# Moving the second unit's queries and norm, and closing the last tile in column halves

## The chip, the cores and the metric

The kernel runs on one core of a Trainium2 chip. The metric is the device time of one execution in microseconds. Before the change it is 1306.41 us, the median of three runs (1306.41 to 1306.56).

## The reference

The reference is a transformer block with modulation. A condition vector c gives six rows (`sa, ca, ga, sb, cb, gb`). Attention runs over 2048 queries and a cache of 2048 keys, with 32 query heads and 8 key and value heads; a gated spatial MLP follows:

```python
mod = (silu(c) @ w_mod)              # 6 rows of 512: sa, ca, ga, sb, cb, gb
h = layernorm(x) * (1 + ca) + sa     # x: 2048 x 512
q = (h @ wq)                         # 32 heads of 128; 4 query heads share a key head
p = softmax(q k^T / sqrt(128))
x = x + ga * ((p v) @ wo)
h = layernorm(x) * (1 + cb) + sb
z = gelu(h @ w_in)                   # 2048 x 1792
z1, z2 = z[:, :896], layernorm(z[:, 896:])
g = w_sp @ z2 + b_sp                 # w_sp: 2048 x 2048
out = x + gb * ((z1 * g) @ w_out)
```

All inputs and the output are bf16.

## The kernel before

The work is an order written out by hand (`tc.manual_schedule()`): each engine and each DMA queue gets its instructions in the order in which the program emits them, and semaphores tie the engines together. The DMAs of this part are all issued by SP, one after the other; the output is written by DMAs that ACT issues.

**Attention.** The 2048 rows of x are 16 tiles of 128 rows, and four tiles are a chunk (`CT = 4`). A unit `u` is one key head and one tile of queries with four query heads: 128 units, unit 0 to 15 for the first key head. The main loop steps through `it`, with eight slots `i` in each. In a slot the program emits, in this order: what was entered for that slot with `at(it, slot, fn)`; the scores of unit `it` (`qk`, L1068: two matmuls of 512 columns into a two-bank PSUM tile `s_ps`, then one exponential of 128x1024 on ACT, L1075); one part of the product with v of an earlier unit (`pv`, L1124: eight matmuls of 129 columns); and what was entered in `fill[it, slot]`, which is mostly query projections (`qproj`, L967). At the end of each group of query heads a cast on DVE (L978) brings the projected queries from PSUM into `qT`. `pv` of unit 0 runs in the last four slots of unit 0 and the even slots of unit 1; after each two heads DVE takes a reciprocal (L1135) and writes the normalised output `onorm` (L1136), and after the fourth head SP transposes it into `oT` (L1147). The projection with wo uses `oT` some units later.

**The first layernorm.** The first chunk's tiles are normalised in the preamble and in unit 0. For the second chunk, `ln1_at(1, (0, 7), (1, 2), (2, 2))` enters four steps: the statistics of its four tiles at slot 7 of unit 0 (`ln1_stats`, L697 and L698 on DVE, then L678 and L682 on POOL for the reciprocal deviation); the normalisation of the four tiles at slot 2 of unit 1 (`ln1_norm`, L686 on DVE); four DMA transposes into `hT` at slot 3 (`ln1_dma`, L836 on SP); and the modulation at slot 2 of unit 2 (`ln1_dma_mod`, four operations on DVE, L805, each over all four tiles). The projection of the second chunk's queries starts in `fill[2, 5]`. Between these, SP loads `wmod_b` (2 MB, L1312, the tile is called `wsp` in the profile), which is entered at slot 4 of unit 1 and is first used in unit 6.

**Queries of unit 2 and 3.** `rest_q` projects tiles 2 and 3 of the first chunk: sixteen matmuls of 256 columns in two groups of two heads, put into the slots 1 to 6 of unit 1. Unit 2's scores need both groups' casts.

**The end.** The last 512 rows of the spatial product are computed as 384 and then 128 columns. For each of seven f the last 128 columns take sixteen matmuls (L1545), one for the bias (L1565), and DVE's product with z1 into `yT` (L1573). The last tile's output projection `o2_mm` (L1578) takes seven matmuls of 512 columns, one for each f: f = 0 to 2 within the loop, f = 3 to 6 behind it. `finish_tile` then multiplies by `gb_rows` from PSUM into `tmp` (L1590), adds x into `yout` (L1591), both on DVE, and ACT issues the DMA (L1592). A flag `redo`, computed earlier, decides at the very end (L1643) whether a general path runs; here it doesn't.

Of the kernel before, what the change touches and what calls it, by code (L numbers as in the profile page):

```python
# [10 lines left out]
BF16 = mybir.dt.bfloat16  # L11
FP32 = mybir.dt.float32
ACT = mybir.ActivationFunctionType
ALU = mybir.AluOpType
AX = mybir.AxisListType
P = 128
# [559 lines left out]
def kernel(  # L576
# [19 lines left out]
    nc = tc.nc  # L596
    _, S, D = A_x.shape
# [7 lines left out]
    NT = S // P  # L605
    NDT = D // P
    NKT = SK // P
    NFT = FH // P
    NCH = S // 512
    CT = 512 // P  # L610
# [8 lines left out]
    out_dram = out[0].rearrange("(t p) d -> p t d", p=P)  # L619
# [26 lines left out]
    x_sb = res.tile([P, NT, D], BF16, name="x_sb")  # L646
    ga_rows = res.tile([P, D], FP32, name="ga_rows")
    gb_rows = res.tile([P, D], FP32, name="gb_rows")
# [20 lines left out]
    def bank(name):  # L669
        return psum.tile([P, 512], FP32, name=name)  # L670
# [4 lines left out]
    def rstd_of(mv, n, tag):  # L675

        ve = stat.tile([P, CT], FP32, name=f"ve_{tag}")
        nc.gpsimd.tensor_scalar(  # L678
            out=ve[:, :n], in0=mv[:, :, 1], scalar1=LN_EPS, scalar2=None, op0=ALU.add
        )  # L680
        rstd = stat.tile([P, CT], FP32, name=f"rstd_{tag}")
        nc.gpsimd.tensor_tensor(out=rstd[:, :n], in0=ve[:, :n], in1=mhalf[:, :n], op=ALU.pow)  # L682
        return rstd

    def normalise(dst, src, mv, rstd):
        nc.vector.tensor_scalar(  # L686
            out=dst,
            in0=src,
            scalar1=mv,
            scalar2=rstd,  # L690
            op0=ALU.subtract,
            op1=ALU.mult,
        )

    def ln_stats(mv, j, src):
        st = stat.tile([P, 1, nc.vector.BN_STATS_DIM], FP32, name="bnst")
        nc.vector.bn_stats(out=st[:, 0, :], in_=src)  # L697
        nc.vector.bn_aggr(out=mv[:, j, :], in_=st[:])  # L698
# [87 lines left out]
    def ln1_stats(j0, n):  # L786
        for j in range(j0, j0 + n):
            ln_stats(mv1, j, x_sb[:, j, :])
        return rstd_of(mv1[:, j0 : j0 + n, :], n, "ln1")

    def ln1_norm(j0, n, rstd):
        xns = []
        for j in range(j0, j0 + n):
            xn = res.tile([P, D], BF16, name="xn1", bufs=4)
            normalise(xn[:], x_sb[:, j, :], mv1[:, j, 0:1], rstd[:, j - j0 : j - j0 + 1])
            xns.append(xn)
        return xns

    def hT_of(ch):
        if ch not in hTs:  # L800
            hTs[ch] = res.tile([P, NDT, 512], BF16, name="hT", bufs=NCH)
        return hTs[ch]

    def ln1_mod(dst, src, dt, engine=nc.vector):
        engine.tensor_scalar(  # L805
            out=dst,
            in0=src,
            scalar1=modc[:, NDT + dt : NDT + dt + 1],
            scalar2=modc[:, dt : dt + 1],
            op0=ALU.mult,  # L810
            op1=ALU.add,
        )
# [20 lines left out]
    def ln1_dma(j0, n, xns):  # L833
        hT = hT_of(j0 // CT)
        for jj in range(n):
            nc.sync.dma_start_transpose(out=hT[:, :, jj * P : (jj + 1) * P], in_=xns[jj][:])  # L836

    def ln1_dma_mod(ch):
        for dt in range(NDT):
            ln1_mod(hTs[ch][:, dt, :], hTs[ch][:, dt, :], dt)  # L840
# [79 lines left out]
    for dt in range(NDT):  # L920
        dst, src = hTs[0][:, dt, 0:P], xT0[:, dt * P : (dt + 1) * P]
        if dt == 1:
            nc.scalar.activation(
                out=dst,
                in_=src,
# [29 lines left out]
    def qproj(b, heads, c0, n, banks=("misc", "misc")):  # L955

        g, ch = divmod(b, NCH)
        if b not in qTs:
            qTs[b] = early.tile([P, REP, 512], BF16, name="qT")
        one = n * len(heads) <= 512  # L960
        ps = {}

        def mm(hh, dt):
            if dt == 0 and (not one or hh == heads[0]):
                ps[0] = bank(banks[hh % 2])
            o0 = (hh - heads[0]) * n if one else 0
            nc.tensor.matmul(  # L967
                ps[0][:, o0 : o0 + n],
                lhsT=wqs[g][:, dt, hh * DH : (hh + 1) * DH],
                rhs=hTs[ch][:, dt, c0 : c0 + n],  # L970
                start=(dt == 0),
                stop=(dt == NDT - 1),
            )
            if dt == NDT - 1 and (not one or hh == heads[-1]):
                hs = heads if one else [hh]
                dst = qTs[b][:, hs[0] : hs[-1] + 1, c0 : c0 + n]
                src = ps[0][:, 0 : len(hs) * n].rearrange("p (h q) -> p h q", q=n)
                nc.vector.tensor_copy(out=dst, in_=src)  # L978

        return [lambda hh=hh, dt=dt: mm(hh, dt) for hh in heads for dt in range(NDT)]  # L980

    first = {}
# [30 lines left out]
    def at(it, slot, fn):  # L1013
        later.setdefault((it, slot), []).append(fn)
# [265 lines left out]
    fill = {}  # L1280
# [16 lines left out]
    fill[0, 4], fill[0, 5] = next_q[0:8], next_q[8:16]  # L1297
    rest_q = qproj(0, [0, 1], 2 * P, 2 * P) + qproj(0, [2, 3], 2 * P, 2 * P)
    for i in range(6):
        fill[1, i + 1] = rest_q[(8 * i + 2) // 3 : (8 * i + 10) // 3]  # L1300

    def ln1_at(ch, stats, norm, turn):
        st = {}
        at(*stats, lambda: st.update(r=ln1_stats(ch * CT, CT)))
        at(*norm, lambda: st.update(x=ln1_norm(ch * CT, CT, st["r"])))
        at(norm[0], norm[1] + 1, lambda: ln1_dma(ch * CT, CT, st["x"]))
        at(*turn, lambda: ln1_dma_mod(ch))

    ln1_at(1, (0, 7), (1, 2), (2, 2))
    ln1_at(2, (2, 4), (3, 1), (4, 5))  # L1310
    ln1_at(3, (3, 5), (4, 1), (5, 5))
    at(1, 4, lambda: nc.sync.dma_start(out=wmod_b, in_=wmod_dram[:, :, 2 * D : NMOD]))  # L1312
# [34 lines left out]
    for g in range(1, HKV):  # L1347
# [7 lines left out]
        last = it - 1  # L1355
        for from_it, load in loads:
# [3 lines left out]
            last = next(u for u in pauses if u >= it + from_it and u > last)  # L1360
# [94 lines left out]
    for it in range(NU + 6):  # L1455
# [37 lines left out]
        if it == NU + 2:  # L1493
            free_b.close()
            mlp = fast.enter_context(tc.tile_pool(name="mlp", bufs=1, side="right"))
            zs["z1T"] = mlp.tile([P, NFT, S], BF16, name="z1T")
            wout_sb = mlp.tile([P, NFT, D], BF16, name="wout_sb")
# [14 lines left out]
    for f in range(NFT):  # L1512
# [6 lines left out]
        out=ok1[:], in0=rall[:], scalar1=1.0 / SAFE, scalar2=None, op0=ALU.is_ge  # L1519
# [8 lines left out]
        out=bad[:], in0=okm[:], scalar1=-1.0, scalar2=1.0, op0=ALU.mult, op1=ALU.add  # L1528
# [48 lines left out]
    def o2_mm(dst, yT, jj, f):  # L1577
        nc.tensor.matmul(  # L1578
            dst,
            lhsT=yT[:, f, jj * P : (jj + 1) * P],  # L1580
            rhs=wout_sb[:, f, :],
            start=(f == 0),
            stop=(f == NFT - 1),
        )

    def finish_tile(t, jj, src):
        j = t * CT + jj
        tmp = mlp.tile([P, D], FP32, name="tmp", bufs=2)[:].bitcast(BF16)[:, 0:D]
        yout = mlp.tile([P, D], BF16, name="yout", bufs=2)
        nc.vector.tensor_tensor(out=tmp[:], in0=src, in1=gb_rows[:], op=ALU.mult)  # L1590
        nc.vector.tensor_tensor(out=yout[:], in0=tmp[:], in1=x_sb[:, j, :], op=ALU.add)  # L1591
        nc.scalar.dma_start(out=out_dram[:, j, :], in_=yout[:])  # L1592
# [3 lines left out]
    def o2_tile(t, jj):  # L1596
        o2 = bank("o_ps")
        for f in range(NFT):
            o2_mm(o2[:], yTs[t], jj, f)
        finish_tile(t, jj, o2[:])  # L1600

    last = NCH - 1
# [16 lines left out]
    o2_last = [acc[jj // 2][:, (jj % 2) * 512 : (jj % 2 + 1) * 512] for jj in range(CT)]  # L1619
    yT = yTs[last]  # L1620
    for f in range(NFT):
        spatial(last, yT, f, 0, n_a)
        if f < CT:
            o2_tile(last - 1, f)
        if f > 0:
            for jj in range(CT - 1):
                o2_mm(o2_last[jj], yT, jj, f - 1)
    redo = nc.values_load(flag[0:1, 0:1], min_val=0, max_val=P)
    for f in range(NFT):
        spatial(last, yT, f, n_a, P, bias_by_pe=True)  # L1630
        if f == 0:
            for jj in range(CT - 1):
                o2_mm(o2_last[jj], yT, jj, NFT - 1)
        elif f < CT:
            o2_mm(o2_last[CT - 1], yT, CT - 1, f - 1)
        if f % 2 == 0 and f < 2 * (CT - 1):
            finish_tile(last, f // 2, o2_last[f // 2])
    for f in range(CT - 1, NFT):
        o2_mm(o2_last[CT - 1], yT, CT - 1, f)
    finish_tile(last, CT - 1, o2_last[CT - 1])  # L1640
    fast.close()

    with tc.If(redo != 0):  # L1643
# [34 lines left out]
```

## Time and profile before

| | value |
|---|---|
| median of 3 runs | 1306.41 us |
| the profiled execution's own time | 1306.41 us |
| its span, first to last instruction | 1304.6 us |
| time around the span | 1.8 us |
| PE busy | 1287.9 us, 99% of the span |
| ACT busy | 1113.4 us, 85% |
| DVE busy | 684.1 us, 52% |
| POOL busy | 57.4 us, 4% |
| mean granted TensorE clock | 0.999 |

PE is the matrix engine, PEld its weight loads, ACT the scalar engine, DVE the vector engine, POOL GpSimd and SP the engine whose queue issues DMAs; a q behind an engine's name means its queue. In a timeline line the columns are the start in us from the begin of the span, the length in us, the engine, the line of the kernel, the operation, the tile written and the tiles read, the shape, and the number of instructions merged into the line; brackets give the idle time before the first of them and what ended it. Durations of matmuls are those of one alone (0.38 us at 512 columns), while back to back they start 0.215 us apart.

### The profile page before, as it was taken

The page shows a single profiled execution, that of the slowest core. Times are in us where ns is not written, and L with a number is a line of the kernel's source. Part 1 is how long each engine was busy: PE and PEld are TensorE (multiplying, and loading weights), DVE is VectorE, ACT ScalarE, POOL GpSimd, SP SyncE. Part 2 cuts the span into 40 slices and gives each one's busy share as a digit, 9 for nine tenths or more (in the row PEclk, how much of TensorE's full clock was granted, in tenths as well). Part 3 has the DMA queues.
Part 4 walks back from the last instruction along what each step waited for, and adds up shares of the span by engine and source line. Part 5 has one row for each costly group of instructions (what it writes and reads, how often), then busy time and mean ns, then how long its engine had stood idle before and what let it go on. Part 6 is the DMA issues. An engine that isn't in the chain of part 4 may idle for free.

```text
span 1304.6 us, 22478 instructions
## 1 busy us (share of the span) xinstructions
PE 1287.9 (99%) x8472; PEld 698.1 (54%) x8626; DVE 684.1 (52%) x1772; ACT 1113.4 (85%) x1683; POOL 57.4 (4%) x93
## 2 busy tenths in 40 slices
PE   8999999999999999999999999999999999999998
PEld 6655555555555555555555555555555556644445
DVE  5635445544554455445544554455445566784443
ACT  7999999999999999999999999999999998650000
POOL 1000000000000000000000000000000133410000
PEclk9999999999999999999999999999999999999999
DMA  7899899999999999999999999999999983264300
GB/s 187 183 198 189 157 190 182 190 170 189 181 194 168 188 173 184 183 181 183 185 188 173 183 187 189 172 185 176 177 198 163 168 151 90 49 137 98 81 21 31
DMA packets 774982, 211.19 MB, mean 162 GB/s; under 512 B 759248, under 2 KB 773200, under 8 KB 774864
## 3 DMA queue, kind: packets, MB, share of 16 engines
q1 hardware_dynamic: 772416, 207.55, 87.0%
q10 hardware_dynamic: 2448, 2.10, 0.5%
q8 instruction: 70, 1.15, 0.4%
q14 instruction: 48, 0.39, 0.1%
HBM read 21.37 MB, written 2.10 MB: 18 GB/s over the span
## 4 chain that ended last, share of the span: by engine, by line
PE 95%; DVE 2%; ACT 1%; DMA 1%; issue 1%; POOL 0%; SPq 0%; ACTq 0%
PE s_ps L1031 21%; PE o_ps L1103 20%; PE o_ps L1124 14%; PE s_ps L1068 13%; PE misc L1181 8%; PE misc L967 8%; PE misc L1545 7%; PE o_ps L1578 1%; PE s_ps L1411 1%; PE s_ps L1372 1%; DVE stz L1394 1%; PE s_ps L1578 0%; DMA wmod_a<-in_w_mod_dram 0%; ACT pT L1075 0%; DMA xnT<-xn 0%
## 5 line engine op out<-in xcount | busy, mean ns | idle before, releaser
L1031 PE MATMUL s_ps<-kT,qT 128*128 128x512 bf16 x1219 | 364.9, 379 | 2.3
L1038 ACT ACTIVATE win_sb<-s_ps 128x1024 bf16<-128x1024 f32 x312 | 319.2, 1024 | 3.8 <-PE s_ps L1031 0.7
L1103 PE MATMUL o_ps<-pT,v 128*128 128x512 bf16 x909 | 272.5, 379 | 1.3
L1174 DVE SCALAR_TENSOR_TENSOR xacc<-misc,rall,xacc 128x512 f32<-128x512 f32 x304 | 227.4, 748 | 68.2 <-PE misc L1181 60.7
L1068 PE MATMUL s_ps<-qT,kT 128*128 128x512 bf16 x784 | 233.2, 379 | 1.9 <-ACT pT L1075 1.1
L1075 ACT ACTIVATE pT<-s_ps 128x1024 bf16<-128x1024 f32 x216 | 217.8, 1025 | 12.9 <-PE s_ps L1068 4.9
L1038 ACT ACTIVATE pn<-s_ps 128x1024 bf16<-128x1024 f32 x208 | 213.0, 1024 | 2.0 <-PE s_ps L1031 0.5
L1103 PEld LDWEIGHTS <-v 128*128 128x128 bf16 x1248 | 122.1, 98 | 147.3
L1075 ACT ACTIVATE wsp<-s_ps 128x1024 bf16<-128x1024 f32 x176 | 179.9, 1024 | 12.1 <-PE s_ps L1068 4.2
L1181 PE MATMUL misc<-wo_g,oT 128*128 128x512 bf16 x479 | 181.5, 379 | 1.0
L967 PE MATMUL misc<-hT,wq_g 128*128 128x512 bf16 (+2 forms) x499 | 179.6, 370 | 0.5
L1031 PEld LDWEIGHTS <-qT 128*128 128x128 bf16 x1248 | 121.5, 98 | 109.4 <-issue 0.4
L978 DVE CAST qT<-misc 128x512 bf16<-128x512 f32 x127 | 87.2, 687 | 151.2 <-PE misc L967 151.2
L1124 PEld LDWEIGHTS <-pT 128*128 128x128 bf16 x1792 | 119.6, 98 | 50.5
L1092 DVE TENSOR_TENSOR tot<-rs 128x1 f32<-128x1 f32 x312 | 48.4, 155 | 171.5 <-ACT win_sb L1038 115.2
L1124 PE MATMUL o_ps<-v,pT 128*128 128x129 bf16 x1792 | 137.5, 220 | 0.6
L1068 PEld LDWEIGHTS <-kT 128*128 128x128 bf16 x784 | 75.6, 98 | 83.0 <-DVE qT L978 1.5
L1124 PEld LDWEIGHTS <-wsp 128*128 128x128 bf16 x1408 | 94.3, 98 | 41.5
L1124 PE MATMUL o_ps<-v,wsp 128*128 128x129 bf16 x1408 | 108.5, 220 | 0.5
L1038 ACT ACTIVATE wmod_a<-s_ps 128x1024 bf16<-128x1024 f32 x104 | 106.4, 1024 | 0.4 <-PE s_ps L1031 0.4
L1545 PE MATMUL misc<-wsp,z 128*128 128x512 bf16 (+2 forms) x554 | 100.1, 336 | 0.4
L1103 PE MATMUL o_ps<-wsp,v 128*128 128x512 bf16 x292 | 87.8, 379 | 0.4
(111 smaller groups left out, 874.3 us busy)
## 6 DMA issues: line engine op xcount, KB each, us to landing
wo_g<-in_A_wo_dram SPq DMA_DIRECT2D x8, 512.0 KB, 5.0
wq_g<-in_A_wq_dram SPq DMA_DIRECT2D x7, 512.0 KB, 4.0
v<-in_A_v_cache_dram SPq DMA_DIRECT2D x7, 512.0 KB, 4.5
wsp<-in_w_mod_dram SPq DMA_DIRECT2D x1, 2048.0 KB, 8.7
out_dram<-yout ACTq DMA_DIRECT2D x16, 128.0 KB, 1.7
pT<-win_sb SPq DMA_TRANSPOSE x117, 4.8
win_sb<-in_B_w_in_dram SPq DMA_DIRECT2D x1, 1792.0 KB, 8.0
x_sb<-in_A_x_dram SPq DMA_DIRECT2D x3, 512.0 KB, 7.0
```

The source lines that it names most:

```text
L967: nc.tensor.matmul(ps[0][:, o0 : o0 + n], lhsT=wqs[g][:, dt, hh * DH : (hh + 1) * DH], rhs=hTs[ch][:, dt, c0 : c0 + n], start=(dt == 0), s ...
L978: nc.vector.tensor_copy(out=dst, in_=src)
L1031: nc.tensor.matmul(s_ps[:, c * 512 : (c + 1) * 512], lhsT=qTs[b][:, hh, jj * P : (jj + 1) * P], rhs=groups[g]["kT"][:, k0 : k0 + 512], sta ...
L1038: nc.scalar.activation(out=rows_of(u, hh)[:, half * HK : (half + 1) * HK], in_=s_ps[:], func=ACT.Exp, scale=inv_sqrt_dh, accum_out=rsums[u ...
L1068: nc.tensor.matmul(s_ps[:, h * 512 : (h + 1) * 512].rearrange("p (r q) -> p r q", r=REP), lhsT=groups[g]["kT"][:, kt * P : (kt + 1) * P], ...
L1075: nc.scalar.activation(out=pTs[u][:, 2 * i : 2 * i + 2, :], in_=s_ps[:].rearrange("p (k q) -> p k q", k=2), func=ACT.Exp, scale=inv_sqrt_dh,)
L1092: nc.vector.tensor_tensor(out=tot[:], in0=rs[:, 2 * hh : 2 * hh + 1], in1=rs[:, 2 * hh + 1 : 2 * hh + 2], op=ALU.add)
L1103: nc.tensor.matmul(o_pss[u][:], lhsT=groups[g]["v1"][:, kt, 0:DH], rhs=pTs[u][:, kt, :], start=(kt == 0), stop=(kt == NKT - 1),)
L1124: nc.tensor.matmul(o_ps[:, hh % 2, 0 : DH + 1], lhsT=pTs[u][:, kt, hh * P : (hh + 1) * P], rhs=groups[g]["v1"][:, kt, 0 : DH + 1], start=( ...
L1174: nc.vector.scalar_tensor_tensor(out=xa[:], in0=X_ps[:], scalar=scale, in1=xa[:], op0=ALU.mult, op1=ALU.add)
L1181: nc.tensor.matmul(ps[0][:], lhsT=oTs[u][:, hh, :], rhs=groups[g]["wo"][:, hh, :], start=(hh == 0 or each), stop=(hh == REP - 1 or each),)
L1545: nc.tensor.matmul(g_pss[f][:, :n], lhsT=z2[:, st, f * P : (f + 1) * P], rhs=wsp[t][:, st, c0 : c0 + n], start=(st == 0), stop=(st == NT - ...
```

## The change

There are two edits, one at each end of the kernel.

In the second unit (unit 1) the projections `rest_q` move from slots 1 to 6 into slots 0 to 5. The statistics of the second chunk stay at slot 7 of unit 0. Its normalisation, which was in one piece at slot 2, is done in two: two tiles at slot 3 and two at slot 6. The four transposes by DMA move from slot 3 to slot 7, and the modulation stays at slot 2 of unit 2.

In the end, the last tile's output projection is made in two halves of 256 columns, each in a PSUM bank of its own, with their own order for f = 3 to 6. DVE multiplies both halves, then POOL adds x to the first half and DVE to the second, and one DMA writes both.

```diff
     for i in range(6):
-        fill[1, i + 1] = rest_q[(8 * i + 2) // 3 : (8 * i + 10) // 3]
+        fill[1, i] = rest_q[(8 * i + 2) // 3 : (8 * i + 10) // 3]
...
-    ln1_at(1, (0, 7), (1, 2), (2, 2))
+    at(0, 7, lambda: first.update(r=ln1_stats(CT, CT)))
+    at(1, 3, lambda: first.update(x=ln1_norm(CT, 2, first["r"])))
+    at(1, 6, lambda: first.update(y=ln1_norm(CT + 2, 2, first["r"][:, 2:CT])))
+    at(1, 7, lambda: ln1_dma(CT, CT, first["x"] + first["y"]))
+    at(2, 2, lambda: ln1_dma_mod(1))
     ln1_at(2, (2, 4), (3, 1), (4, 5))
     ln1_at(3, (3, 5), (4, 1), (5, 5))
     at(1, 4, lambda: nc.sync.dma_start(out=wmod_b, in_=wmod_dram[:, :, 2 * D : NMOD]))
...
+    halves = [slice(hf * D // 2, (hf + 1) * D // 2) for hf in range(2)]
+    o2_half_ps = [o2_last[CT - 1][:, 0 : D // 2], bank("o_ps")[:, 0 : D // 2]]
+    def o2_half(hf, f):
+        nc.tensor.matmul(
+            o2_half_ps[hf],
+            lhsT=yT[:, f, (CT - 1) * P : CT * P],
+            rhs=wout_sb[:, f, halves[hf]],
+            start=(f == 0),
+            stop=(f == NFT - 1),
+        )
...
         elif f < CT:
-            o2_mm(o2_last[CT - 1], yT, CT - 1, f - 1)
+            for hf in range(2):
+                o2_half(hf, f - 1)
...
-    for f in range(CT - 1, NFT):
-        o2_mm(o2_last[CT - 1], yT, CT - 1, f)
-    finish_tile(last, CT - 1, o2_last[CT - 1])
+    for hf, f in ((0, 3), (0, 4), (0, 5), (1, 3), (1, 4), (0, 6), (1, 5), (1, 6)):
+        o2_half(hf, f)
...
+    for hf in range(2):
+        nc.vector.tensor_tensor(
+            out=tmp[:, halves[hf]], in0=o2_half_ps[hf], in1=gb_rows[:, halves[hf]], op=ALU.mult
+        )
+    for hf, engine in ((0, nc.gpsimd), (1, nc.vector)):
+        engine.tensor_tensor(
+            out=yout[:, halves[hf]],
+            in0=tmp[:, halves[hf]],
+            in1=x_sb[:, j_end, halves[hf]],
+            op=ALU.add,
+        )
+    nc.scalar.dma_start(out=out_dram[:, j_end, :], in_=yout[:])
```

More of the change, by code (lines that the diff above doesn't have):

```diff
@@ L1634 @@
         elif f < CT:
-            o2_mm(o2_last[CT - 1], yT, CT - 1, f - 1)
+            for hf in range(2):
+                o2_half(hf, f - 1)
         if f % 2 == 0 and f < 2 * (CT - 1):
             finish_tile(last, f // 2, o2_last[f // 2])
-    for f in range(CT - 1, NFT):
-        o2_mm(o2_last[CT - 1], yT, CT - 1, f)
-    finish_tile(last, CT - 1, o2_last[CT - 1])
+    for hf, f in ((0, 3), (0, 4), (0, 5), (1, 3), (1, 4), (0, 6), (1, 5), (1, 6)):
+        o2_half(hf, f)
+    j_end = NT - 1
+    tmp = mlp.tile([P, D], FP32, name="tmp", bufs=2)[:].bitcast(BF16)[:, 0:D]
+    yout = mlp.tile([P, D], BF16, name="yout", bufs=2)
+    for hf in range(2):
[10 more added lines that the diff above has]
+    nc.scalar.dma_start(out=out_dram[:, j_end, :], in_=yout[:])
     fast.close()
```

## The prediction

> **What bounds the kernel now.** I read the page first (shares, chain), then the timeline of the second and third unit (17 to 36 us) and of the last 10 us, SP's queue over the first stretch, who waited for whom up to 60 us, and the tile view of hT. The page:
>
> ```profile
> PE 1287.9 (99%) x8472; PEld 698.1 (54%) x8626; DVE 684.1 (52%) x1772; ACT 1113.4 (85%) x1683; POOL 57.4 (4%) x93
> PE 95%; DVE 2%; ACT 1%; DMA 1%; issue 1%; POOL 0%; SPq 0%; ACTq 0%
> ```
>
> PE is the kernel: an edit is worth what it does to PE's start times at that place, because nothing later has room to give it back. Around the first edit the timeline shows:
>
> ```profile
> 18.88 7.66 ACT L1075 ACTIVATE pT<-s_ps 128x1024 bf16<-128x1024 f32 x8
> ...
> 23.36 1.38 DVE L686 TENSOR_SCALAR xn<-x_sb,mv,rstd_ln 128x512 bf16<-128x512 bf16 x4 [0.98 <-POOL rstd_ln L682]
> ...
> 25.79 0.68 DVE L978 CAST qT<-misc 128x512 bf16<-128x512 f32 x1
> 26.53 0.61 PE L1068 MATMUL s_ps<-qT,kT 128*128 128x512 bf16 x2 [1.05 <-ACT pT L1075]
> ...
> 27.23 5.60 ACT L1075 ACTIVATE pT<-s_ps 128x1024 bf16<-128x1024 f32 x6 [0.70 <-PE s_ps L1068]
> ...
> 31.04 1.38 DVE L805 TENSOR_SCALAR hT<-hT,modc 128x512 bf16<-128x512 bf16 x4 [4.57 <-DMA hT<-xn]
> ...
> 31.94 0.59 PE L967 MATMUL misc<-hT,wq_g 128*128 128x512 bf16 x2
> ```
>
> In unit 1 ACT is the pace (8 exponentials in 7.66 us). The last query cast sits on DVE behind four normalisations; unit 2's first scores wait for it, PE stands 1.05 us and ACT 0.70. Then DVE stands 4.57 us for the transposed second chunk, and PE takes up that chunk's projection at 31.94, only 0.45 us after its first modulated part was ready (31.04 + 0.41, plus some 0.05 to PE). That is all the room the second chunk has. SP's queue shows what delivers it:
>
> ```profile
> 12.24 0.50 SPq L738 DMA_DIRECT2D wo_g<-in_A_wo_dram  x1
> 23.80 5.90 SPq L836 DMA_TRANSPOSE hT<-xn  x4
> 29.75 0.59 SPq L1312 DMA_DIRECT2D wsp<-in_w_mod_dram  x1
> 30.43 1.25 SPq L1147 DMA_TRANSPOSE oT<-onorm  x1
> ```
>
> SP issues in program order, and a transpose occupies it while it is issued: 1.96 us for the first of these four, 1.21 to 1.22 for the others, with 0.09 between. Each lands 2.44 us after its issue begins (the first 3.06).
>
> **Queries up a slot.** Sixteen matmuls of 256 columns (0.107 us apart) begin in slot 0 instead of 1. Slot 0 then issues scores at 18.21, PV at 18.64, three projections at 19.09 (their hT is ready at 18.66), and slot 1's scores at 19.41 instead of 19.09; they end at 20.0, so ACT's second exponential starts near 20.05 instead of 19.83: minus 0.22 us. The first cast goes ahead of the norm (DVE free at 22.3), the second follows its first half: norm 23.36 to 24.01 (the rstd still comes from POOL at 23.32), cast 24.01 to 24.69. Unit 2's first scores then wait for ACT alone and ACT's 0.70 us hole goes. By itself this is a gain of 0.70 - 0.22 = 0.48 us in an ACT-paced stage.
>
> **The norm in two parts, its DMAs behind.** Tiles 2 and 3 are normalised at slot 6 (24.61 to 25.28), then come the reciprocal (0.20) and the onorm (0.42) of unit 0's second pair of heads: done at 25.90, against 25.87 now. Splitting costs DVE nothing. The queue is another matter. The four transposes move from slot 3 to slot 7, and so behind two other DMAs on SP.
>
> The first is the 2 MB load of wmod_b (slot 4). It waits for no computed data: it has been held only by the transposes ahead of it. Now SP can issue it right after wo_g, near 12.8. The DMA engines are almost idle from 20 to 24 us (shares 0.02 and 0.04); the load moves in about 5.5 us (381, 414 and 284 GB/s in three 2 us stretches from 32 us), so it follows wo_g and is done near 26. I cost it at nothing; its cover is that idle stretch. Were it late by x, the transposes would land late by x.
>
> The second is oT of unit 0 (slot 6), which waits for the onorm. Now it is the one that stands behind; after the change hT stands behind it, though oT is needed only in unit 4. SP: oT from 25.95; it is now the first transpose after SP's long rest, so I give it 1.96 us: 27.91. The four hT follow at 1.31 each: 28.00, 29.31, 30.62, 31.93; the last lands at 34.37, against 30.91. Bounds for the slow one: in the three series of four hT here (from 23.80, 38.58 and 48.75) one transpose in each took 0.58 to 0.75 us longer, without a cause I can name; none slow gives 33.6, a second slow one 35.1. I take one, as in each series.
>
> DVE's modulation waits at its head for all four; queued behind it are unit 1's reciprocals, the statistics of chunk 2 and the casts. It starts at 34.50 (0.13 after landing, as before), its first two parts are done at 34.91 and 35.23, PE's two projections start at 34.96 and 35.28, and the next scores at 35.49 against 32.37: plus 3.1 us. PE would have come there at 31.4, so it stands some 3.4 us; the 0.48 us gained before ends in this wait. DVE itself is late by 3.46; the third query head waits for the bank that the first cast (36.08 to 36.74 now) frees, and has 0.42 us of slack there (it starts at 37.21), so 3.12 + 0.42 covers 3.46 and nothing is added. Everything behind moves along: chunk 2's transposes landed at 45.5 for use at 48.99, and the load that stood ahead of them is gone. Bounds of the whole step: plus 2.4 (no slow transpose) to plus 3.9.
>
> **The last tile in halves.**
>
> ```profile
> 1299.10 0.10 PEld L1578 LDWEIGHTS <-yT 128*128 128x128 bf16 x1 [0.23 <-DVE yT L1573]
> 1299.62 0.69 DVE L1590 TENSOR_TENSOR tmp<-s_ps,gb_rows 128x512 bf16<-128x512 f32 x1 [0.57 <-PE s_ps L1578]
> 1300.34 0.42 DVE L1591 TENSOR_TENSOR yout<-tmp,x_sb 128x512 bf16<-128x512 bf16 x1
> ```
>
> Twice the matmuls at half the columns is the same PE time (weight loads, about 0.06 us apart in the 128-column series, stay under 0.107). After the wait for the last yT (1299.15), three half matmuls remain instead of two halves' worth: the first half ends at 1299.42, the second near 1299.64, 0.06 later than the whole does now. DVE: tmp half one 1299.46 to 1299.88 (0.42, the row of 128x256 from PSUM, onorm), half two to 1300.28. [...] DVE's add of half two (0.30, by 0.42 at 512 and 0.36 at 384 columns) would end at 1300.60, but it reads two SBUF operands, and such a one is held beside POOL:
>
> ```profile
> 1025.11 1.27 POOL L1197 TENSOR_TENSOR xacc<-xacc,ga_rows 128x512 f32<-128x512 f32 x1 [165.43 <-DVE xacc L1168]
> 1026.01 0.39 DVE L1092 TENSOR_TENSOR tot<-rs 128x1 f32<-128x1 f32 x1
> ```
>
> tot takes 0.15 elsewhere; here it ended 0.02 after POOL (twice more, at 1052.13 and 1060.83), while onorm, with PSUM as one source, ran unhindered. So DVE ends near 1300.61 + 0.17 = 1300.78, against 1300.76 now. Not held: minus 0.15; POOL slower (0.85 us): plus 0.2. I take 0.0.
>
> **Sum.** The profiled execution took 1306.41 us (span 1304.6 and 1.8 around it), the median of the runs. 1306.4 + 3.1 + 0.0 = 1309.5, that is 0.24% slower. About 0.2%, 2.6 us, is what a measurement of this kernel can tell from no change; the bounds 2.4 and 3.9, with 0.2 either way for the tail, lie on both sides of it: 1308.6 to 1310.5.
>
> **Rivals.** *The second chunk comes in time* (not slower). Place: SP's queue in unit 1. It decides when the last transpose lands before about 31 us, 3.4 us earlier than I have it: if the four hT were issued ahead of oT after all, or SP issued them without 1.31 us each. For it: the first two tiles are ready at 24.0. Against it: SP keeps program order throughout this trace, and all twelve hT transposes of the program took 1.21 us or more, whatever the state of the queue. Then the 0.48 us stay: 1305.9. Chance 0.12. Part of this (one or two transposes ahead, 1307 to 1308.4): 0.05.
>
> *PE loses its fast clock in the new hole.* The program's first eleven 512-column matmuls start 0.427 us apart (1.18 to 5.42 us), later ones 0.215, under a granted clock of 1.00 in both, so PE does run at half rate when it starts cold. The only long idle stretch since, 1.05 us, changed nothing (0.61 us for the next pair); 3.4 us is not to be seen here. Falling back costs half of a stretch like that first one (4.2 us): plus 2.1, 1311.6. Chance 0.08. [...]
>
> **How the numbers follow.** Forecast, the late second chunk: 0.75, at 1309.5. The range leaves out the clock's fall and the gain and keeps 0.8: 1307.3 to 1310.9. Slower by over 0.2% (above 1309.0): two thirds of the forecast's 0.75, since only the case without a slow transpose falls below, and the 0.08 of the clock: 0.58. Within 0.2%: the rest of these and the second chunk in time: 0.40. A gain of 2.6 us is more than all the idle PE time in these stages: 0.02.
>
> **What would show it.** Right: the wmod_b load issued near 13 us; SP with oT ahead of four hT from about 26 us; DVE's wait before L805 longer than 4.57 us, near 8; PE idle some 3 us before L967 near 35 us; no wait of 1.05 us at the first scores of unit 2; the end's DVE add ending with or just after POOL's. Wrong: hT ahead of oT on SP, L805 starting near 31, or a spacing of 0.427 us in the matmuls behind the hole.

## The result and the profile after

The changed kernel takes 1310.46 us, the median of 9 runs (1309.21 to 1310.98), against 1306.41 us, the median of 9 runs of the kernel before (1306.34 to 1306.94). The ratio is 1.003 with a 95% interval of 1.0019 to 1.004: 4.05 us slower. The forecast was 1309.5 us, slower, in a range of 1307.3 to 1310.9.

The page of the profile says that PE is still the kernel:

```profile
PE 1296.8 (99%) x8633; PEld 699.0 (53%) x8633; DVE 684.9 (52%) x1773; ACT 1113.0 (85%) x1683; POOL 57.7 (4%) x94
```

PE's busy time can't be compared with the 1287.9 us of before: that trace has 8626 weight loads but only 8472 of the matmuls, this one has both.

The timeline around the first edit, after the change (start, length, engine, line, operation, tiles, shape, count, idle time before it):

```profile
21.75 12.19 ACT L1075 ACTIVATE pT<-s_ps 128x1024 bf16<-128x1024 f32 x13 [0.16 <-PE s_ps L1068]
...
27.57 0.59 PE L1068 MATMUL s_ps<-qT,kT 128*128 128x512 bf16 x2 [0.32 <-ACT pT L1075]
...
35.52 1.38 DVE L805 TENSOR_SCALAR hT<-hT,modc 128x512 bf16<-128x512 bf16 x4 [7.85 <-DMA hT<-xn]
35.99 0.70 PE L967 MATMUL misc<-hT,wq_g 128*128 128x512 bf16 x2 [2.79 <-DVE hT L805]
...
37.16 1.02 ACT L1075 ACTIVATE pT<-s_ps 128x1024 bf16<-128x1024 f32 x1 [3.22 <-PE s_ps L1068]
```

The hole before unit 2's first scores has shrunk to 0.32 us of PE from 1.05, and ACT runs 13 exponentials without a break. But DVE now waits 7.85 us for the transposed second chunk instead of 4.57, PE stands 2.79 us before that chunk's projection (no hole before), and ACT 3.22 us. SP's queue shows why:

```profile
13.33 1.19 SPq L1316 DMA_DIRECT2D wsp<-in_w_mod_dram  x1
27.70 1.24 SPq L1147 DMA_TRANSPOSE oT<-onorm  x1
28.98 5.19 SPq L836 DMA_TRANSPOSE hT<-xn  x4
```

The 2 MB load goes out at 13.33, oT stands ahead of the four transposes, and they begin at 28.98 (23.80 before).

All times of this execution carry an offset from before the edit. I compared the starts of ACT's exponentials one by one with those of before: unit 0 is already 1.69 us late (12.10 instead of 10.40), unit 2's scores then 1.07, the exponentials behind the hole 4.15, and those from there to the end of ACT's work between 4.06 and 4.6. So the edit adds 2.46, and 1.69 lies in the preamble, whose instructions the change doesn't touch. A part of it is a load that landed later. The first matmuls on `wmod_a`, in the profile of before and then of after:

```profile
6.18 0.35 PE L874 MATMUL misc<-sc_bf,wmod_a 128*128 128x1 bf16 x8
...
6.76 0.35 PE L874 MATMUL misc<-sc_bf,wmod_a 128*128 128x1 bf16 x8 [1.74 <-DMA wmod_a<-in_w_mod_dram]
```

That is 0.58 us. The other 1.11 come behind it, and the windows of the trace show what slowed PE there (columns: stretch and length, then busy time and count of PE, PEld, DVE, ACT and POOL, then PEclk, DMA share, GB/s):

```profile
6.00:8.00 2.00, 1.24 (x28) 0.96 (x29) 0.00 (x0) 0.00 (x0) 0.00 (x0) 0.81 1.12 354
8.00:10.00 2.00, 2.00 (x19) 1.17 (x17) 0.88 (x4) 0.29 (x1) 0.21 (x1) 0.50 1.53 284
10.00:12.00 2.00, 1.76 (x21) 1.59 (x19) 1.47 (x5) 0.57 (x2) 0.27 (x1) 0.83 0.93 177
```

From 7.25 to 10.66 us PE was granted half its clock; in the profile of before PEclk is 1.00 there. At the end of the kernel:

```profile
1303.78 0.42 DVE L1661 TENSOR_TENSOR tmp<-s_ps,gb_rows 128x256 bf16<-128x256 f32 x1 [0.38 <-PE s_ps L1636]
1304.34 0.67 POOL L1665 TENSOR_TENSOR yout<-tmp,x_sb 128x256 bf16<-128x256 bf16 x1 [122.07 <-SPq L1674]
1304.57 0.58 DVE L1665 TENSOR_TENSOR yout<-tmp,x_sb 128x256 bf16<-128x256 bf16 x1
```

DVE's add takes 0.58 us and ends 0.15 behind POOL's.

That leaves two questions. Is the loss really that of SP's order? And where does the rest of the 4.05 us come from in most executions, if the order gives about 2.5?

### The profile page after: what moved, and what is told of

Its sections match the earlier page's. It is cut to its first block, busy times and chain, and to the rows that moved or that the text cites. A ratio compares the mean times of both kernels' runs of the same rounds, so it can differ in the third digit from the quotient of the medians.

```text
span 1309.1 us, 22649 instructions
## 1 busy us (share of the span) xinstructions
PE 1296.8 (99%) x8633; PEld 699.0 (53%) x8633; DVE 684.9 (52%) x1773; ACT 1113.0 (85%) x1683; POOL 57.7 (4%) x94
## 4 chain that ended last, share of the span: by engine, by line
PE 97%; DVE 1%; DMA 1%; SPq 0%; ACT 0%; POOL 0%; issue 0%; DVEq 0%
PE o_ps L1103 21%; PE s_ps L1031 21%; PE o_ps L1124 13%; PE s_ps L1068 12%; PE misc L1181 8%; PE misc L967 8%; PE misc L1549 7%; PE s_ps L1376 2%; PE s_ps L1415 2%; PE o_ps L1582 1%; DMA wmod_a<-in_w_mod_dram 0%; PE s_ps L1582 0%; SPq L836 0%; ACT pT L1059 0%; DMA hT<-xn 0%; DVE bnst L697 0%
## 5 line engine op out<-in xcount | busy, mean ns | idle before, releaser
L1031 PE MATMUL s_ps<-kT,qT 128*128 128x512 bf16 x1248 | 371.4, 379 | 0.1
L1103 PE MATMUL o_ps<-pT,v 128*128 128x512 bf16 x944 | 280.3, 379 | 0.0
L1181 PE MATMUL misc<-wo_g,oT 128*128 128x512 bf16 x512 | 194.2, 379 | 0.1
L967 PE MATMUL misc<-hT,wq_g 128*128 128x512 bf16 (+2 forms) x528 | 190.7, 371 | 2.8 <-DVE hT L805 2.8
L1103 PE MATMUL o_ps<-wsp,v 128*128 128x512 bf16 x304 | 90.5, 380 | 0.0
```

Of the source, the lines that this page charges most:

```text
L967: nc.tensor.matmul(ps[0][:, o0 : o0 + n], lhsT=wqs[g][:, dt, hh * DH : (hh + 1) * DH], rhs=hTs[ch][:, dt, c0 : c0 + n], start=(dt == 0), s ...
L1031: nc.tensor.matmul(s_ps[:, c * 512 : (c + 1) * 512], lhsT=qTs[b][:, hh, jj * P : (jj + 1) * P], rhs=groups[g]["kT"][:, k0 : k0 + 512], sta ...
L1103: nc.tensor.matmul(o_pss[u][:], lhsT=groups[g]["v1"][:, kt, 0:DH], rhs=pTs[u][:, kt, :], start=(kt == 0), stop=(kt == NKT - 1),)
L1181: nc.tensor.matmul(ps[0][:], lhsT=oTs[u][:, hh, :], rhs=groups[g]["wo"][:, hh, :], start=(hh == 0 or each), stop=(hh == REP - 1 or each),)
```

## The experiments

There are ten experiments, each run beside the kernel before. My theory: PE waits for the second chunk, because oT and the later norm hold its transposes on SP. Rivals: the end costs part of it; the early 2 MB load delays the transposes. For the rest I had two theories, named from e5 on: G, the hole lets PE fall to its slow clock; P, the preamble alone does.

**One edit at a time.** e1 is the kernel before with the first edit alone (the first two pieces of the change's diff) and so with the old end.

> Only the first edit (queries, norm and transposes of unit 1); the end is that of the kernel before. Theory (the second chunk's transposes stand behind oT on SP, PE waits for them): the whole loss is here, PE idle about 2.8 us before L967 near 34 to 36 us, and 2.5 to 2.8 us over the kernel before (1309.0 to 1309.2), plus up to 1.7 us if the preamble falls to the slow PE clock as in the profile of after (first exponential of unit 0 at 12.1 instead of 10.4). Rival (the end in halves costs part of it, by POOL and the branch behind it): at least 0.5 us less than the changed kernel in like preambles.

Measured: 1310.25 us, the median of 7 (1308.45 to 1310.71), ratio 1.0029 (1.0018 to 1.004). Its profiled execution is the fastest of the seven and shows the hole alone, with a granted clock of 1.00 in every stretch from 4 to 50 us:

```profile
33.42 1.38 DVE L805 TENSOR_SCALAR hT<-hT,modc 128x512 bf16<-128x512 bf16 x4 [7.86 <-DMA hT<-xn]
33.89 0.70 PE L967 MATMUL misc<-hT,wq_g 128*128 128x512 bf16 x2 [2.80 <-DVE hT L805]
34.42 0.59 PE L1068 MATMUL s_ps<-qT,kT 128*128 128x512 bf16 x2
```

The scores behind the hole come at 34.42 instead of 32.37: 2.05 us, and that execution is 2.04 us over the kernel before's 1306.41, less than the 2.5 to 2.8 that I expected. But its unit 0 began early: the first exponential starts at 9.99, 0.41 us ahead of the profile of before. Counted from there the edit costs 2.46 us, as in the profile of after; the same working gives 2.46 in e5 and e6 too. The other six lie between 1309.69 and 1310.71, so there are two groups, with about 1.8 us between them.

e2 is the other half: the start of before (`fill[1, i + 1]`, `ln1_at(1, (0, 7), (1, 2), (2, 2))`) and the new end.

> Only the second edit (last tile in halves); the start is that of the kernel before. Theory: within 0.2 us of the kernel before, 1306.3 to 1306.7, DVE's last add held to end some 0.15 us behind POOL's. Rival (the end costs): 1307 or more. If the slow PE clock in the preamble came from the first edit, it stays away here (1306.4); if it comes from any change of the program, it shows here too, with about 1.7 us more.

Measured: 1306.36 us, the median of 11 (1306.05 to 1306.64), ratio 0.9999 (0.999 to 1.0008). The end is worth nothing either way, and no second group shows.

**The order on SP.** e3 keeps both edits and puts the four transposes ahead of oT (`ln1_dma_at` is a new helper, `ln1_dma` for the tiles from the third of the chunk on):

```diff
...
     at(1, 3, lambda: first.update(x=ln1_norm(CT, 2, first["r"])))
+    at(1, 5, lambda: ln1_dma(CT, 2, first["x"]))
     at(1, 6, lambda: first.update(y=ln1_norm(CT + 2, 2, first["r"][:, 2:CT])))
-    at(1, 7, lambda: ln1_dma(CT, CT, first["x"] + first["y"]))
+    at(1, 6, lambda: ln1_dma_at(CT, 2, 2, first["y"]))
```

> The changed kernel, but the transposes of the second chunk ahead of oT on SP: two tiles at slot 5 of unit 1, two at slot 6 right behind their norm. Theory: last transpose issued near 28.0 and landed near 30.5 (1.7 us later each if the preamble is slow), PE reaches L967 without a hole, and the first edit's gain of about 0.5 us shows: 1305.7 to 1306.1 with a fast preamble, up to 1.7 us more with a slow one. Rival (the 2 MB load of wmod_b, now early, or the order of DVE makes the second chunk late): the hole of 2 us or more before L967 stays, 1308 or more with a fast preamble.

Measured: 1305.96 us, the median of 11 (1305.62 to 1306.64), ratio 0.9997 (0.9988 to 1.0006). The last transpose landed at 30.66, PE has no hole before the projection (L973 in this kernel), and no execution is in the second group:

```profile
26.91 2.53 SPq L842 DMA_TRANSPOSE hT<-xn  x2
...
30.79 1.38 DVE L805 TENSOR_SCALAR hT<-hT,modc 128x512 bf16<-128x512 bf16 x4 [5.09 <-DMA hT<-xn]
...
31.26 0.70 PE L973 MATMUL misc<-hT,wq_g 128*128 128x512 bf16 x2
```

The early load did no harm: it still goes out at 12.5.

e7 changes only oT's place; the norm and the four transposes stay where the change put them:

```diff
-            if by_rows(it):
+            if by_rows(it) or u == 0:
                 at(it + 1, 0, turn)
```

> The changed kernel with oT of unit 0 issued one slot later, at slot 0 of unit 2, and so behind the four transposes on SP; the norm stays in two parts at slots 3 and 6. Theory: the transposes start when the second half's norm is done (25.3 with a fast preamble) instead of 26.9, the hole shrinks from 2.8 to 1.2 us, or 1.9 if one transpose takes 0.7 longer: 1306.8 to 1307.6, and by theory G no slow group, since 1.2 us is little more than the hole of 1.05 us that the kernel before has. Rival (the load of wmod_b is what is ahead): as the changed kernel, 1308.4 or more.

Measured: 1306.09 us, the median of 11 (1305.81 to 1307.24), ratio 0.9999 (0.999 to 1.0008). Better than the 1306.8 to 1307.6 that I expected, and the queue shows my error:

```profile
12.47 1.20 SPq L1316 DMA_DIRECT2D wsp<-in_w_mod_dram  x1
23.75 5.63 SPq L836 DMA_TRANSPOSE hT<-xn  x4
29.48 1.22 SPq L1147 DMA_TRANSPOSE oT<-onorm  x1
```

The transposes do not begin when the second half of the norm is done, but at 23.75, with the first half: entered in one slot, they still wait one by one, each for its own tile. So slot 7 alone costs nothing. Of what stands ahead of them, oT alone makes the hole: oT waits for an onorm that is done at 25.94, 2 us after the first tile's transpose began.

e6 puts the load back behind the transposes (`at(1, 4, ...)` of wmod_b becomes `at(1, 7, ...)`), so that only oT is ahead.

> The changed kernel with the 2 MB load of wmod_b put back behind the four transposes on SP, so that only oT of unit 0 stands ahead of them. Theory (oT and the later norm hold the transposes, the early load is hidden in the idle DMA stretch): as the changed kernel, hole before L967 2.8 us, up to 0.7 more if the first transpose of the program is a slow one, fastest execution 1308.4 to 1309.4, most near 1310.4. Rival (the early load delays the transposes): the hole shrinks by 1 us or more, fastest near 1307.5.

Measured: 1310.29 us, the median of 9 (1308.74 to 1310.71), ratio 1.0028 (1.0018 to 1.0038):

```profile
25.70 1.24 SPq L1147 DMA_TRANSPOSE oT<-onorm  x1
26.98 5.20 SPq L836 DMA_TRANSPOSE hT<-xn  x4
32.23 0.59 SPq L1316 DMA_DIRECT2D wsp<-in_w_mod_dram  x1
```

The hole is 2.79 us, as in the changed kernel, so the early load has no part in it. Three executions lie at 1308.74 to 1308.78, six at 1310.09 to 1310.71: the two groups again.

**The rest: PE's clock.** e5 feeds PE while it stands, with matmuls ahead of the second chunk's projection:

```diff
+    def feed(n):
+        f_ps = bank("misc")
+        for k in range(n):
+            nc.tensor.matmul(
+                f_ps[:], lhsT=wqs[0][:, 0, 0:P], rhs=hTs[0][:, 0, :], start=True, stop=True
+            )
+    fill[2, 5] = [lambda: feed(10)]
```

> The changed kernel with ten more 512-column matmuls on PE in the hole before the second chunk's projection (slot 5 of unit 2), on data that is there; their result is thrown away. At 0.215 us each they fill 2.15 of the 2.8 us for which PE stands and should move nothing. Theory G (the 1.7 us by which most executions of the changed kernel and of the run with the first edit alone lie above their fastest come from PE falling to its slow clock in or behind the hole): all executions now lie at 1308.4 to 1309.4, the slow group is gone. Theory P (they come from the preamble's clock and have nothing to do with the hole): two groups as before, the median stays near 1310.4.

Measured: 1308.65 us, the median of 11, ratio 1.0019 (1.001 to 1.0028); ten of the eleven lie between 1308.46 and 1308.87, one at 1310.20, outside what I expected.

```profile
31.24 2.11 PE L1347 MATMUL misc<-hT,wq_g 128*128 128x512 bf16 x9
33.51 1.38 DVE L805 TENSOR_SCALAR hT<-hT,modc 128x512 bf16<-128x512 bf16 x4 [7.85 <-DMA hT<-xn]
33.98 0.70 PE L967 MATMUL misc<-hT,wq_g 128*128 128x512 bf16 x2 [0.64 <-DVE hT L805]
```

DVE waits as long as before and PE reaches the projection at the same time, but the idle time is filled (nine of the ten matmuls are in the record; 0.64 us are left), and the upper group vanishes but for one execution. Ten matmuls more make the kernel 1.8 us faster than the changed one. That is theory G's result.

e8 is the changed kernel again, for its trace:

> The changed kernel once more, for its trace alone. Theory G: if this execution is one of the slow group, matmuls of 512 columns behind the hole start 0.427 us apart for some us and the granted clock shows under 1.00 there, between 36 and 45 us. Theory P: the slow stretch lies between 7 and 11 us, as in its first profile, and the matmuls behind the hole start 0.215 us apart.

Measured: 1310.69 us, and this execution caught the fall (the same columns as the windows above):

```profile
34.00:36.00 2.00, 1.79 (x8) 0.84 (x8) 1.97 (x7) 0.11 (x1) 0.00 (x0) 0.67 0.01 4
36.00:38.00 2.00, 2.00 (x11) 1.10 (x10) 1.90 (x7) 0.91 (x1) 0.00 (x0) 0.50 0.00 0
38.00:40.00 2.00, 1.95 (x21) 1.36 (x21) 1.90 (x6) 1.28 (x2) 0.97 (x2) 0.97 0.00 0
```

PE was idle for 2.81 us, from 31.40 to 34.21. The granted clock is 0.67 in the first of these stretches, 0.50 in the second and 0.97 in the third, which at one half makes some 1.3, 2.0 and 0.1 us, 3.4 in all; its 512-column matmuls start 0.43 us apart there (two of them from 34.79 to 35.65). Half of 3.4 us is 1.7, about the distance of the two groups; counted from unit 0, the exponentials behind the slow stretch are 4.14 us late, 1.68 more than the 2.46 of the order. The preamble was not slowed in this execution: PEclk is 1.00 in every stretch from 4 to 34 us.

The executions without a trace have a mean granted clock in the result, to three digits. One stretch of 3.41 us at one half, as in the first profile, takes 0.0013 off it. Fifteen executions are listed at 0.998, and all of them belong to upper groups: seven of the changed kernel's eight, three of e1's six, four of e6's six, and e8. No other execution is listed so, neither the lower ones nor any of the 76 of the kernel before beside the experiments, nor the 77 of e2, e3, e4, e5, e7, e9 and e10. The remaining six of the upper groups are listed at 0.999, which rounding leaves open. As the preamble is the same in all these kernels, theory P doesn't explain the groups, though a fall there does occur, as the first profile shows (0.50 from 7.25 to 10.66 us). And e5's execution at 1310.20 is listed at 1.0, which leaves no room for a fall of 3.41 us: what made it late is not shown.

**The parts that gain.** e4 is the kernel before with `fill[1, i]` for `fill[1, i + 1]` and nothing else.

> The kernel before with the queries of unit 1 up a slot and nothing else. Theory: DVE's two casts still follow the whole norm (24.65), the second ends near 25.9 instead of 26.5, unit 2's first scores no longer wait for it and ACT's 0.70 us hole shrinks to 0.1; the transposes stay where they were, so no new hole: 0.3 to 0.6 us faster, 1305.8 to 1306.1, with a fast preamble. Rival (ACT's new bubble in slot 1 and the order of DVE eat it): within 0.1 us of the kernel before.

Measured: 1305.76 us, the median of 11 (1305.38 to 1305.91), ratio 0.9995 (0.9986 to 1.0004). That is just below what I expected. The wait before unit 2's first scores falls to 0.44 us, and PE takes up L967 at 31.17 without a hole:

```profile
25.76 0.60 PE L1068 MATMUL s_ps<-qT,kT 128*128 128x512 bf16 x2 [0.44 <-DVE qT L978]
...
31.17 0.59 PE L967 MATMUL misc<-hT,wq_g 128*128 128x512 bf16 x2
```

e9 repeats it on another chip:

> The kernel before with the queries of unit 1 up a slot, a second time, to see whether its gain holds on another chip: 1305.5 to 1305.9, 0.6 us under the kernel before, no execution above 1306.2.

Measured: 1305.78 us, the median of 11 (1305.5 to 1306.2; one at 1306.20 touches my bound), the kernel before 1306.37, ratio 0.9996 (0.9987 to 1.0005). e10 adds the norm in two parts, with oT behind the transposes as in e7, and the old end:

> The first edit alone with oT of unit 0 put behind the four transposes, and the end of the kernel before. Theory (the norm in two parts is worth nothing more than the queries' move, since ACT paces units 1 and 2 either way): 1305.6 to 1306.1, within 0.3 us of the queries' move alone. Rival (the cast, which now comes ahead of the second half of the norm, is worth more): 0.3 us or more under it.

Measured: 1305.97 us, the median of 11 (1305.75 to 1307.12), ratio 0.9998 (0.9989 to 1.0007). The norm in two parts adds nothing to the queries' move.

The best version is therefore the queries' move alone. Its 22 executions lie at 1305.38 to 1306.20, and the 50 of the kernel before beside them at 1305.83 to 1306.74: the medians are 0.68 and 0.59 us lower, and in both traces ACT's exponentials of unit 2 come 0.53 to 0.54 us earlier, counted from unit 0. The intervals of the ratio include 1, so by them the gain stays open.

## Why the prediction was right, and where not

**The end: right.** Forecast 0.0 by DVE's last add held until POOL's ends plus 0.17; measured 0.15 behind POOL, and e2 took 1306.36 against 1306.44 of the kernel before beside it. The end of POOL's add at 1300.61, on which the 0.0 stands, was reckoned with 0.15 us of fixed cost that no run shows; what the runs show is an add of 0.67 us for 128x256 in after and e2, where 128x512 took 1.16 in before.

**The queries: right.** Forecast 0.48 gained before the hole; ACT's exponentials of unit 2 come 0.62 us earlier relative to unit 0 in the profile of after, and e4, where no hole follows, keeps 0.54 by its trace and 0.68 by its median.

**The order on SP: the mechanism right, the size too large.** oT ahead of four transposes, the load out near 13 us, DVE's wait near 8 us (7.85): all as written. The term was plus 3.1 and measured 2.46, counted from unit 0, in the traces of after, e1, e5 and e6. The step that was mis-sized is the slow transpose: I charged the first one 1.96 us, as the first transpose after SP's long rest, because each series of the trace had a slow one. Here oT took 1.24 and the four 1.27 or less, spaced 1.31 as forecast, in all five traces with oT first. That is 0.72 us less, which accounts for the difference of 0.66 within 0.06. PE stood 2.8 us and not 3.4 for the same reason. My own bound without a slow transpose, plus 2.4, was the value. Nor is the first transpose always slow where the four go first: it took 1.24 in e4 and e9, 1.47 in e2, 1.71 in e7 and 1.96 to 1.99 in the kernel before, e3 and e10. What makes one transpose slow in some series stays open.

Of the reasons that I gave for the four being late, e7 and e6 keep one: oT. The move to slot 7 and the 2 MB load that overtook them cost nothing.

**PE's clock: a rival that came true, its chance wrong.** I priced it at 2.1 us and gave it 0.08; it costs 1.68. It happens in most executions: 8 of 9 of the changed kernel, 6 of 7 of e1 and 6 of 9 of e6 lie in the upper group, though one of these (the first profile) fell in the preamble. The granted clock of 1.00 that I read beside the first eleven matmuls is none: in the trace of before the first entry of the clock is its rise at 6.20 us, and the view shows 1.00 ahead of it. Their spacing of 0.427 us was the better sign. The chance of 0.08 was my estimate and rests on no run: the only hole that I could compare with, 1.05 us in the profile of before, changed nothing, and that said nothing of one of 2.8. In e8 a hole of 2.81 us was followed by about 3.4 us at half the clock.

So the total came near by two errors of opposite sign: 0.66 us too much for the order, and 1.68 too little for the clock in most executions. 1306.41 + 2.46 + 1.68 is 1310.55, and the median is 1310.46. That this median lies in my range is in part luck: the range was meant to leave the clock's fall out, and it reached so far up only because the order was charged 0.66 us too much; without that its upper end would be about 1310.2. The rival in which the second chunk comes in time gave 1305.9, and e3 and e10, in which it does, measured 1305.96 and 1305.97.

## What to carry to other kernels

oT, a DMA that waits for computed data, held back the four transposes that were emitted behind it on SP's queue (behind oT they began at 26.88 in e1, ahead of it at 23.75 in e7): when a step moves, read the queue's order from the old slot to the new one, and ask of each DMA passed both what it waits for and how soon its result is needed (oT was needed two units later than hT). And a hole on PE is not priced by its length alone: that of 2.81 us in e8 was followed by about 3.4 us at half the clock as well, that of 2.80 in e1 was not, and with ten matmuls thrown into the hole (0.64 us left in e5) ten of eleven executions stayed at or under 1308.87 us.

## What the runs showed of the hardware

Two traces show a granted clock of one half ahead of the last matmul: the first profile of after for 3.41 us, from 7.25 to 10.66, and e8 for about 3.4 us between 34 and 40. In the trace of before PEclk is 1.00 from its rise at 6.20 until 1303.20 us; in the next 0.1 us it is 0.84. The last matmul had ended at 1299.57, 3.6 us earlier.

Holes of nearly the same length were followed by half the clock in one trace and by the full one in three. In e8 PE was idle for 2.81 us, and PEclk was 0.67 in 34 to 36 us and 0.50 in 36 to 38. In e1 (2.80 us idle), in e6 (2.79) and behind the hole of the first profile of after (2.79) it was 1.00 in every stretch up to 50 us. It was 1.00 also behind the 1.05 us of before and the 0.64 us that are left in e5. In the preamble of the first profile of after PE was idle for 1.74 us, from 5.02 to 6.76, then ran one-column matmuls, and PEclk was 0.50 from 7.25 to 10.66. So a hole of 2.8 us was followed by a loss of 1.68 us in e8 and by none in the other three traces, and what decided it is not shown. That the fall explains each execution of the upper groups is inferred from e5, from the traces and from the listed clocks; where in the other executions the clock fell is not shown.

A DVE add of two SBUF tiles beside a POOL add ended behind POOL's again, 0.15 us behind in the changed kernel and 0.14 in e2. It took 0.58 us for 128x256 in both, where I had put an unheld one at 0.30; the add of 128x512 with POOL idle took 0.42 in before.
